# Attention in front of two expert layers: the pieces of the global rows move to another accumulation bank

## The chip, the cores and the metric

The kernel runs on one core of a Trainium2 chip. TensorE (PE in the profile, with PEld for its weight loads) multiplies matrices into PSUM, an accumulation memory of 8 banks; VectorE (DVE), ScalarE (ACT) and GpSimd (POOL) work element by element; SyncE (SP) issues the transfers. Each engine takes its own instructions in order, and engines wait for each other by semaphores. The metric is the device time of one execution in microseconds.

## The reference

Local rows attend to 32 global keys and to local keys within 32 positions; global rows attend to everything. Two dense layers follow: one with a leaky activation, and one with eight experts of equal capacity.

```python
k_all = np.concatenate([k_g, k_l], axis=2)
v_all = np.concatenate([v_g, v_l], axis=2)
s_g = scale * np.matmul(q_g, k_all.transpose(0, 1, 3, 2))
out_g = np.matmul(sm(s_g), v_all)
...
mask = np.abs(pos[:, None] - pos[None, :]) <= window
s_ll = np.where(mask, s_ll, -1000000000.0)
s_l = np.concatenate([s_lg, s_ll], axis=-1)
out_l = np.matmul(sm(s_l), np.concatenate([v_g, v_l], axis=2))
...
h = x @ w_in
g = np.maximum(h, 0.0) + alpha * np.minimum(h, 0.0)
x = g @ w_out
```

There are 4 batches of 8 heads, 512 local and 32 global rows each, with a head size of 64.

## The kernel before

A *unit* is a batch and two heads. Two units make a pair p, 8 in all, and a pair takes four steps j = 0 to 3; the running step is n = 4 p + j, from 0 to 34. What is issued in a step is written out by hand for TensorE, VectorE and ScalarE in `attention()`, so that each step works on several steps' data. In step n:

- `scores(p, j)`: the local scores of step n go into two banks `s` (L456). VectorE reduces them in four pieces, scaling, masking and taking the least (L462, an instruction and a read of its accumulator each); ScalarE exponentiates (L466).
- `dense.products(n)`: from step 12 on, half a column block of the first dense layer (h, L684, later L692), so that TensorE has other work.
- `wide_part(n)`: the global rows. They take a whole pair's four steps. j = 1: the pair's global scores, 512 columns in a bank of their own and 32 more (`gscores`, L522), their least (L529) and their exponential (L533). j = 3: the exponentials are transposed, four blocks in an own bank and two in `s` (`gtrans`, L545), and copied to `gt` (L546). j = 0 of the next pair: their product with the values (`gpv`, L555, 24 matmuls, each recorded as two in the trace), scaled on VectorE into `go` (L558). j = 2: that is turned (`gturn`, L565) and copied to the output (L566). All parts but the two with own banks use columns 256 to 511 of the *second scores bank* of the running step, `G[p]["s"][1]`.
- `pv(n - 2)` (L488), local product of step n - 2, into columns 0 to 255 of a bank `o`, which VectorE normalises in `norm` (L494, L496). `ptrans(n - 1)` (L474) transposes the exponentials of step n - 1, and ScalarE copies them to `pt` (L476). `oturn(n - 3)` (L503) turns the rows of step n - 3 into columns 256 to 511 of the `o` bank of the step before, and VectorE or ScalarE in turn copies them out (L505).

The global pieces leave their VectorE and ScalarE work in a list `soon`, which is emptied right after `wide_part`, before pv and norm. Between these, `fill("V", ...)` puts VectorE's part of the decoding of 64-bit weights (L87 to L94), whose raw blocks the SP queue loads (L80). Before step 12, TensorE also runs a few products of the unit matrix on the new `o` bank (L616). `dense.close` computes `al1` = 1 - alpha (L653) in step 13, from `ag`, which is loaded at L603.

There are two `s` banks from step 8 on, and two `o` banks. A bank `o` is used in its own step and the next, and is free again when the copy L505 of the next step has read it.

Of the kernel before, what the change touches and what calls it, by code (L numbers as in the profile page):

```python
# [9 lines left out]
F32 = mybir.dt.float32  # L10
# [4 lines left out]
AF = mybir.ActivationFunctionType  # L15
OP = mybir.AluOpType
# [3 lines left out]
BIG = 3.0e38  # L20
# [5 lines left out]
def tile_attention_moe_moe(ctx: ExitStack, tc: tile.TileContext, qkw, vw,  # L26
                           w_in, w_out, w_out_t, gate, w1, w2, out):
    nc = tc.nc
    V, A, P, T = nc.vector, nc.scalar, nc.gpsimd, nc.tensor
    B, H, S, D, SG = BHSDG  # L30
# [330 lines left out]
    with ExitStack() as at:  # L361
# [14 lines left out]
        def bank(shape, name):  # L376
            pool, tag = pY, "y"
            if name == "s" and wide[0]:
                pool, tag = pS, "s"
            elif name == "s":  # L380
                pool, tag = ((pS, "s"), (pS, "s"), (pH, "h1"), (pH, "h1"))[turn[0] % 4]
                turn[0] += 1
            elif name in ("t", "gs0", "gt0"):
                pool, tag = pX, "x"
            return pool.tile(shape, F32, name=name, tag=tag)
# [94 lines left out]
        def pv(p, j, o):  # L480
            d = G[p]
            d["o", j] = o
            for pr in range(2):
                for h, c in heads():
                    for w in range(2):
                        i = 4 * j + 2 * pr + w
                        for a in range(2):
                            T.matmul(o[lane(w, a), 128 * pr + D * h:128 * pr + D * h + D], d["t", j][:, 2 * pr + h, lane(w, a)],  # L488
                                     U[2 * p + a]["v"][:, i, c], start=True, stop=True)
# [20 lines left out]
        def glane(a, h):  # L510
            return slice(SG * (2 * a + h), SG * (2 * a + h + 1))

        def gscores(p, part):
            d = G[p]
            if part == 0:
                d["mx"] = gp.tile([128, 4], F32, name="gmx", bufs=2)
            mx = d["mx"]
            s = d["s"][1][:, 256:256 + SG] if part else bank([128, S], "gs0")
            for a in range(2):
                k = U[2 * p + a]["k"]  # L520
                x = k[:, WIN:2 * WIN] if part else k[:, GO:GE + WIN].rearrange("p (m c) -> p m c", c=3 * WIN)[:, :, :2 * WIN]
                T.matmul(s[64 * a:64 * a + 64], U[2 * p + a]["g"], x, start=True, stop=True)  # L522
            if part:
                to, x, z = gsc[:, 2 * WIN:3 * WIN], s, gzero.to_broadcast([128, SG])
            else:
                to = gsc[:, :GE + WIN - GO].rearrange("p (m c) -> p m c", c=3 * WIN)[:, :, :2 * WIN]
                x = s.rearrange("p (m c) -> p m c", c=2 * WIN)
                z = gzero.unsqueeze(2).to_broadcast([128, S // (2 * WIN), 2 * WIN])
            V.tensor_tensor_reduce(out=to, in0=x, in1=z, scale=-D ** -0.5, scalar=mx[:, 0:1] if part else BIG,  # L529
                                   op0=OP.add, op1=OP.min, accum_out=mx[:, part:part + 1])  # L530
            if part:
                d["p"] = gp.tile([128, GE - GO], F32, name="gpr")
                A.activation(out=d["p"], in_=gsc[:, :GE - GO], func=AF.Exp, bias=mx[:, 1:2], scale=-1.0, accum_out=mx[:, 2:3])  # L533
                P.tensor_scalar(mx[:, 2:3], mx[:, 2:3], 1e-9, None, op0=OP.add)
                later.append(lambda: V.reciprocal(mx[:, 3:4], mx[:, 2:3]))

        def gtrans(p, part):
            d = G[p]
            n = 2 if part else 4
            t = d["s"][1][:, 256:].rearrange("p (n q) -> p n q", q=128) if part else bank([128, n, 128], "gt0")  # L540
            if not part:
                d["t"] = gp.tile([128, len(GW), 128], F32, name="gt")
            for i in range(n):
                o = kpos(GW[4 * part + i]) - GO
                T.transpose(t[:, i], d["p"][:, o:o + KW], ident)  # L545
            soon.append(lambda: (V.tensor_copy if part else A.copy)(d["t"][:, 4 * part:4 * part + n], t))  # L546

        def gpv(p, s):
            d = G[p]
            o = s[:, 256:256 + D]  # L550
            for n, w in enumerate(GW):
                r = slice(96 if w == NQ - 2 else 0, 128)
                for h, c in heads():
                    for a in range(2):
                        T.matmul(o[glane(a, h)], d["t"][r, n, glane(a, h)], U[2 * p + a]["v"][r, w, c],  # L555
                                 start=n == 0, stop=n == len(GW) - 1)
            d["o"] = gp.tile([128, D], F32, name="go")
            soon.append(lambda: V.tensor_scalar(d["o"], o, d["mx"][:, 3:4], None, op0=OP.mult))  # L558

        def gturn(p, s):  # L560
            d = G[p]
            o = s[:, 256:256 + 2 * SG]
            i = ident.rearrange("p (a h q) -> p h a q", a=2, h=2)
            for h, r in heads():
                T.matmul(o[r], d["o"], i[:, h], start=True, stop=True)  # L565
            soon.append(lambda: V.tensor_copy(d["x"][:, :, :SG], o.rearrange("p (a q) -> p a q", q=SG)))  # L566
# [10 lines left out]

        later, soon, at_out = [], [], [None]

        def wide_part(n):  # L580
            p, j = divmod(n, STEPS)
            last = n - STEPS * NU // 2
            if last >= 0:
                s = bank([128, 512], "s") if last in (0, 1) else None
            else:
                s = G[p]["s"][1]
            if j == 1 and last < 0:
                gscores(p, 0)
                gscores(p, 1)
            if j == 3:  # L590
                gtrans(p, 0)
                gtrans(p, 1)
            if p and j == 0:
                gpv(p - 1, s)
            if p and (j == 2 or last == 1):
                gturn(p - 1, s)

        def attention():
            N = STEPS * NU // 2
            for n in range(N + 3):  # L600
                p, j = divmod(n, STEPS)
                if n == SOLO - 1:
                    nc.sync.dma_start(out=ag, in_=gate)  # L603
                wide[0] = n >= SOLO
                dense.turn(n)
                if n < N:
                    scores(p, j)
                while later:
                    later.pop(0)()
                dense.close(n)  # L610
                fill("V", 2)
                o = None
                if 2 <= n < N + 2:
                    o = bank([128, 512], "o")
                    for _ in range((2, 0, 2, 2)[j] if n < BEG else 0):
                        T.matmul(o[:, :128], ident, ident, start=True, stop=True)  # L616
                dense.products(n)
                if n < N + 2:
                    wide_part(n)
                while soon:  # L620
                    soon.pop(0)()
                fill("V", 2 if n >= SOLO and n % 3 == 0 else 1 if n < SOLO else 0)
                if 2 <= n < N + 2:
                    v, j2 = divmod(n - 2, STEPS)
                    pv(v, j2, o)
                    norm(v, j2)
                if 1 <= n <= N:
                    ptrans(*divmod(n - 1, STEPS))
                if n >= 3:
                    oturn(*divmod(n - 3, STEPS))  # L630
                if p and j == 3:
                    gout(p - 1)
                if n > 2:
                    fill("A", 2)
                yield 0
            while later:
                later.pop(0)()
            gout(NU // 2 - 1)

        class dense:  # L640
# [8 lines left out]
                dense.over = []  # L649

            def close(n):
                if n == BEG + 1:
                    V.tensor_scalar(al1, al, -1.0, 1.0, op0=OP.mult, op1=OP.add)  # L653
                if n == BEG - 3:
                    dense.x = [gx.tile([128, KD, CH], F32R, name=nm) for nm in ("xh", "xl")]
                    dense.g = [gt_.tile([128, KH, CH], F32R, name=nm, tag=nm) for nm in ("ghi", "glo")]
                if n in (BEG - 2, BEG - 1):
                    k = slice(0, 2) if n == BEG - 2 else slice(2, KD)
                    split(dense.x[0][:, k], dense.x[1][:, k], XB[0][:, k, :CH], lo_eng=P)
                for f, ps, neg in dense.neg:  # L660
                    g = gh_.tile([128, CH], F32, name="g")
                    V.scalar_tensor_tensor(g, neg, al1[:, f:f + 1], ps, op0=OP.mult, op1=OP.add)
                    split(dense.g[0][:, f], dense.g[1][:, f], g, lo_eng=P)
# [157 lines left out]
    with ExitStack() as mo:  # L821
# [903 lines left out]
        for k in range(E):  # L1725
            n = 0.0
# [103 lines left out]
```

## Time and profile before

| | us |
|---|---|
| runs | 803.5, 808.19, 808.4 |
| median | 808.19 |
| profiled execution | 804.26 |
| its span, first to last instruction | 802.2 |
| PE busy | 758.6 (95%) |
| DVE busy | 483.3 (60%) |
| ACT busy | 404.0 (50%) |
| POOL busy | 413.6 (52%) |

The time of an execution holds its span and what lies around it. The attention with its steps takes the first 140 us or so; after it come the first dense layer, the choice of the experts' rows and the second layer. Busy shares are means over all of these.

### The profile page before, as it was taken

To read this page: it belongs to the slowest core of one execution; us is meant where nothing else is said; L and a number is where in the kernel's file an instruction comes from. 1 tells how busy PE (TensorE), PEld (TensorE's weight loads), DVE (VectorE), ACT (ScalarE), POOL (GpSimd) and SP (SyncE) were. 2 spreads that over 40 slices of the span, in tenths; PEclk is the share of its full clock that TensorE was granted. 3 is DMA by queue.
4 is the path that set the end of the run, shared out by engine and by line. 5 is a ranking of instruction groups with operands and counts; after the bars stand their busy time and mean duration, and the time that the engine had idled before them with its cause. 6 is when DMAs were issued, how large, how long until landed. Compare 5 with 4: busy or idle time off the path is not lost. (4 is left out here: it accounts for less than half of the span.)

```text
span 802.2 us, 21108 instructions
## 1 busy us (share of the span) xinstructions
PE 758.6 (95%) x8258; PEld 695.8 (87%) x8258; DVE 483.3 (60%) x1672; ACT 404.0 (50%) x1018; POOL 413.6 (52%) x384
## 2 busy tenths in 40 slices
PE   6888889999999999899999999999999999999996
PEld 4656667999998999798898999998889999999994
DVE  3788887375664754266655566766677777652220
ACT  5787888345544453454565234423555454544430
POOL 2233333023211332865587349355899987788511
PEclk9999999999999999999999999999999999999999
DMA  8989896431434342126543957316466666466510
GB/s 335 317 301 310 304 314 233 168 122 50 125 110 135 107 145 98 57 64 217 196 141 113 322 199 229 97 33 186 140 194 213 206 185 203 139 190 218 172 41 29
DMA packets 59516, 139.56 MB, mean 174 GB/s; under 512 B 5400, under 2 KB 23000, under 8 KB 58393
## 3 DMA queue, kind: packets, MB, share of 16 engines
q1 hardware_dynamic: 56489, 129.30, 49.6%
q0 software_dynamic: 2928, 8.92, 3.1%
q8 instruction: 65, 1.06, 0.5%
q14 instruction: 34, 0.28, 0.1%
HBM read 113.68 MB, written 24.51 MB: 172 GB/s over the span
## 5 line engine op out<-in xcount | busy, mean ns | idle before, releaser
L74 POOL TENSOR_TENSOR m<-raw,m 128x1024 fp32r<-128x1024 f32 x64 | 152.1, 2401 | 10.8 <-ACT m L73 9.6
L74 POOL TENSOR_TENSOR glo<-g,ghi 128x272 fp32r<-128x272 f32 x64 | 55.1, 860 | 137.6 <-ACT ghi L73 119.4
L1427 PE MATMUL h<-xsh,m 128*128 128x272 f32 x512 | 104.6, 294 | 0.7 <-DVE sbs L1193 0.7
L882 PE MATMUL h<-op,quad 128*128 128x272 f32 x672 | 90.4, 294 | 4.3 <-ACT g L907 2.3
L882 PEld LDWEIGHTS h<-op,quad 128*128 128x128 f32 x672 | 86.6, 191 | 8.4 <-ACT g L907 2.8
L73 ACT CAST m<-raw 128x1024 fp32r<-128x1024 f32 x64 | 65.8, 1048 | 54.9 <-DMA raw<-in_moe_w_dram 37.9
L1447 PE MATMUL h<-hh,m 128*128 128x272 f32 x448 | 92.1, 295 | 0.0
L1582 PE MATMUL h<-gr,wh 128*128 128x272 f32 x448 | 90.8, 296 | 0.0
L251 PE MATMUL y<-ghi,wout 128*128 128x272 f32 x448 | 87.0, 290 | 0.5 <-ACT ghi L73 0.5
L211 PE MATMUL h<-xh,win 128*128 128x272 f32 x448 | 86.2, 290 | 0.0
L1427 PEld LDWEIGHTS h<-xsh,m 128*128 128x128 f32 x512 | 82.0, 188 | 1.4 <-DVE sbs L1193 1.0
L1427 PE MATMUL h<-xsl,m 128*128 128x272 f32 x256 | 73.8, 291 | 0.0
L251 PEld LDWEIGHTS y<-ghi,wout 128*128 128x128 f32 x448 | 70.8, 188 | 2.4 <-issue 1.7
L1447 PEld LDWEIGHTS h<-hh,m 128*128 128x128 f32 x448 | 72.1, 189 | 0.4 <-ACT m L73 0.4
L1582 PEld LDWEIGHTS h<-gr,wh 128*128 128x128 f32 x448 | 71.2, 189 | 0.9 <-ACT gr L73 0.4
L211 PEld LDWEIGHTS h<-xh,win 128*128 128x128 f32 x448 | 70.7, 188 | 0.2 <-DVE g L217 0.2
L1447 PE MATMUL h<-hl,m 128*128 128x272 f32 x224 | 66.3, 296 | 0.0
L251 PE MATMUL y<-glo,wout 128*128 128x272 f32 x224 | 64.7, 289 | 1.5 <-POOL glo L74 1.5
L1582 PE MATMUL h<-gr,wl 128*128 128x272 f32 x224 | 65.7, 293 | 0.0
L211 PE MATMUL h<-xl,win 128*128 128x272 f32 x224 | 64.4, 288 | 0.0
L74 POOL TENSOR_TENSOR gr<-gback,gr 128x272 fp32r<-128x272 f32 x48 | 36.2, 778 | 39.9 <-ACT gr L73 39.5
L466 ACT ACTIVATE pr<-pr,mx 128x128 f32<-128x128 f32 x128 | 49.7, 392 | 12.4 <-DVE mx L462 12.4
(326 smaller groups left out, 1775.9 us busy)
## 6 DMA issues: line engine op xcount, KB each, us to landing
raw<-in_moe_w_dram SPq DMA_DIRECT2D x64, 512.0 KB, 3.7
vv<-in_v_dram SPq DMA_DIRECT2D x28, 512.0 KB, 6.3
qk<-in_qk_dram SPq DMA_DIRECT2D x28, 360.0 KB, 7.1
raw<-in_moe_w_in_dram SPq DMA_DIRECT2D x16, 512.0 KB, 3.9
raw<-in_moe_w_out_dram SPq DMA_DIRECT2D x16, 512.0 KB, 3.5
xs<-xb SPq DMA_DIRECT2D x16, 272.0 KB, 6.4
xpart<-xd SPq DMA_DIRECT2D x32, 136.0 KB, 2.5
xb<-xs SPq DMA_DIRECT2D x4, 1088.0 KB
```

Of the source, the lines that this page charges most:

```text
L73: a = A.copy(hi, src)
L74: return a, (lo_eng or V).tensor_tensor(lo, src, hi.bitcast(F32), op=OP.subtract)
L211: T.matmul(ps, WI[w][:, k, fs], x[:, k], start=i == 0, stop=i == 3 * KD - 1)
L251: T.matmul(ps, WO[w][:, f, ds_], x[:, f], start=f == 0 and i == 0, stop=f == KH - 1 and i == 2)
L466: A.activation(out=sc, in_=sc, func=AF.Exp, bias=d["mx", j][:, ii:ii + 1], scale=-1.0, accum_out=d["sm", j][:, ii:ii + 1])
L882: T.matmul(ps, w[a][kk][:, q * 128:(q + 1) * 128], x[:, b, kk], start=fresh and m == 0, stop=m == 5, skip_group_check=not fresh)
L1427: T.matmul(ps, d["w1"][w][:, kk, f * 128:(f + 1) * 128], x[:, kk], start=kk == 0 and i == 0, stop=kk == KD - 1 and i == 2)
L1447: T.matmul(ps, d["w2"][w][f][:, ms], x[:, f], start=i == 0, stop=i == 3 * K3 - 1)
L1582: T.matmul(ps[j], (woh, wol)[w][f][:, ds_], x, start=f == 0 and a == 0, stop=f == KH - 1 and a == 2)
```

## The change

The global pieces are put into columns 256 to 511 of the step's `o` bank, which `wide_part` now gets as an argument; it is taken from step 1 on. The global product is done by units: unit 0 in j = 0 and unit 1 in j = 1, 12 matmuls each, each with its own scaling of 64 partitions. The small part of the global scores is multiplied before pv, the wide part after it. `soon` is emptied after pv and norm. `al1` is computed in step 7 and `ag` is issued in step 1.

```diff
-            s = d["s"][1][:, 256:256 + SG] if part else bank([128, S], "gs0")
+            s = so[:, 480:480 + SG] if part else bank([128, S], "gs0")
...
-            t = d["s"][1][:, 256:].rearrange("p (n q) -> p n q", q=128) if part else bank([128, n, 128], "gt0")
+            t = so[:, 256:].rearrange("p (n q) -> p n q", q=128) if part else bank([128, n, 128], "gt0")
...
-        def gpv(p, s):
+        def gpv(p, s, units_):
...
-                    for a in range(2):
+                    for a in units_:
...
-            soon.append(lambda: V.tensor_scalar(d["o"], o, d["mx"][:, 3:4], None, op0=OP.mult))
+            if units_[0] == 0:
+                d["o"] = gp.tile([128, D], F32, name="go")
+            b = slice(2 * SG * units_[0], 2 * SG * (units_[-1] + 1))
+            soon.append(lambda: V.tensor_scalar(d["o"][b], o[b], d["mx"][b, 3:4], None, op0=OP.mult))
...
+            last = n >= STEPS * NU // 2
+            if p and j < 2 and not (last and j):
+                gpv(p - 1, s, range(2) if last else (j,))
+            if p and j == (1 if last else 2):
+                gturn(p - 1, s)
+            if j == 1 and not last:
+                soon.append(gscores(p, 1, s))
             if j == 3:
                 gtrans(p, 0)
-                gtrans(p, 1)
...
+                gtrans(p, 1, s)
...
-                if n == SOLO - 1:
+                if n == 1:
                     nc.sync.dma_start(out=ag, in_=gate)
...
-                    wide_part(n)
+                    wide_part(n, o)
+                if 2 <= n < N + 2:
+                    pv(*divmod(n - 2, STEPS), o)
+                    norm(*divmod(n - 2, STEPS))
+                if j == 1 and n < N:
+                    soon.insert(0, gscores(p, 0))
                 while soon:
                     soon.pop(0)()
...
-                if 2 <= n < N + 2:
-                    v, j2 = divmod(n - 2, STEPS)
-                    pv(v, j2, o)
-                    norm(v, j2)
...
-                if n == BEG + 1:
+                if n == SOLO - 1:
                     V.tensor_scalar(al1, al, -1.0, 1.0, op0=OP.mult, op1=OP.add)
```

On TensorE, steps 8 and 9 (j = 0 and j = 1 of pair 2) read before, with `s<-vv,gt` the global product, `gs` the wide and `s<-qk 64x32` the small global scores:

```order
L456 MATMUL s<-qk 32x128 x16
L616 MATMUL o<-ident 128x128 x2
L555 MATMUL s<-vv,gt 32x64 x24
L488 MATMUL o<-vv,pt 32x64 x16
L474 MATMUL t<-ident,pr 128x128 x4
L503 MATMUL o<-ident,on 128x128 x2
L456 MATMUL s<-qk 32x128 x16
L522 MATMUL gs_859<-qk 64x512 x2
L522 MATMUL s<-qk 64x32 x2
```

and now:

```order
L456 MATMUL s<-qk 32x128 x16
L616 MATMUL o<-ident 128x128 x2
L558 MATMUL o<-vv,gt 32x64 x12
L488 MATMUL o<-vv,pt 32x64 x16
L474 MATMUL t<-ident,pr 128x128 x4
L503 MATMUL o<-ident,on 128x128 x2
L456 MATMUL s<-qk 32x128 x16
L558 MATMUL o<-vv,gt 32x64 x12
L522 MATMUL o<-qk 64x32 x2
L488 MATMUL o<-vv,pt 32x64 x16
L522 MATMUL gs_883<-qk 64x512 x2
L474 MATMUL t<-ident,pr 128x128 x4
```

Half of the global product has gone to the next step, its bank is `o`, and the wide scores stand behind pv.

On VectorE, step 13 (j = 1 of pair 3) reads before, from the last read of L462 to the first L462 of step 14:

```order
L462 ISA mx 128x1
L653 TENSOR_SCALAR al_71<-ag 128x16
L87 TENSOR_SCALAR mag<-mag 128x512
L90 TENSOR_SCALAR mag<-mag 128x512
L529 ISA gsc,gmx<-gs_1214,gzero 128x8x64
L529 ISA gmx 128x1
L529 ISA gsc,gmx<-s,gzero,gmx 128x32
L529 ISA gmx 128x1
L494 RECIPROCAL sm<-sm 128x4
L496 TENSOR_TENSOR on<-o,sm 128x256
L505 COPY xb<-o 128x4x2x32
L462 ISA pr,mx<-s,mask 128x128
```

and now:

```order
L462 ISA mx 128x1
L87 TENSOR_SCALAR mag<-mag 128x512
L90 TENSOR_SCALAR mag<-mag 128x512
L494 RECIPROCAL sm<-sm 128x4
L496 TENSOR_TENSOR on<-o,sm 128x256
L531 ISA gsc,gmx<-gs_1238,gzero 128x8x64
L531 ISA gmx 128x1
L563 TENSOR_SCALAR go<-o,gmx 64x64
L531 ISA gsc,gmx<-o,gzero,gmx 128x32
L531 ISA gmx 128x1
L505 COPY xb<-o 128x4x2x32
L462 ISA pr,mx<-s,mask 128x128
```

The norm (L494, L496) has moved ahead of the global reductions (now L531), a scaling of unit 1 stands between these, and L653 has left the step.

## Rows read from the trace of the kernel before

**Rows 1.** Windows: stretch, its length, busy us by engine, granted clock, DMA share, GB/s.

```profile
core 0: us, PE busy (x) PEld busy (x) DVE busy (x) ACT busy (x) POOL busy (x), PEclk, DMA share, GB/s
60.00:100.00 40.00, 33.48 (x810) 25.09 (x814) 33.14 (x133) 31.61 (x111) 14.13 (x21) 1.00 0.90 307
100.00:140.00 40.00, 35.62 (x880) 27.37 (x868) 32.94 (x149) 33.78 (x120) 14.65 (x22) 1.00 0.80 273
160.00:300.00 140.00, 137.92 (x1081) 134.39 (x1080) 88.64 (x153) 66.81 (x155) 39.75 (x47) 1.00 0.37 112
```

**Rows 2.** Waits of PE, 22 to 146 us: us in total, times, longest.

```profile
PE o L488 <- issue: 4.1, 3, 1.8
PE s L555 <- ACT pr L466: 2.8, 2, 1.6
PE s L555 <- DVE mx L462: 1.7, 4, 0.6
PE t L474 <- issue: 1.4, 1, 1.4
PE s L565 <- DVE mx L462: 1.4, 4, 0.9
...
PE s L545 <- DVE mx L462: 1.0, 2, 0.7
PE s L456 <- issue: 0.9, 1, 0.9
...
PE s L555 <- ACT mag L85: 0.3, 1, 0.3
```

**Rows 3.** Waits of DVE in the same stretch.

```profile
DVE pr L462 <- PE s L456: 6.9, 13, 1.0
DVE on L496 <- PE o L488: 2.6, 6, 1.0
DVE go L558 <- PE s L555: 2.5, 2, 2.1
...
DVE xb L566 <- PE s L565: 1.0, 2, 0.6
```

**Rows 4.** Timeline of PE, step 16 (j = 0): start, us, instruction, idle before.

```profile
72.76 0.29 PE L684 MATMUL h<-xh,win 128*128 128x272 f32 x1
74.27 1.10 PE L555 MATMUL s<-vv,gt 128*32 128x64 f32 x48 [1.22 <-ACT pr L466]
75.31 0.65 PE L488 MATMUL o<-vv,pt 128*32 128x64 f32 x32
75.89 0.66 PE L474 MATMUL t<-ident,pr 128*128 128x128 f32 x4
```

**Rows 5.** Timeline of DVE, end of step 15 to start of step 17.

```profile
72.87 0.41 DVE L505 COPY xb<-o 128x256 f32<-128x256 f32 x1
...
74.04 0.08 DVE L462 DVE_READ_ACCUMULATOR2_ANT mx<- 128x1 f32 x1
...
75.64 0.17 DVE L494 RECIPROCAL sm<-sm 128x4 f32<-128x4 f32 x1
76.03 0.42 DVE L496 TENSOR_TENSOR on<-o,sm 128x256 f32<-128x256 f32 x1 [0.21 <-PE o L488]
77.40 0.29 DVE L462 CUSTOM_DVE_ANT_0 pr<-s,mask 128x128 f32<-128x128 f32 x1 [0.95 <-PE s L456]
```

**Rows 6.** Groups by line, 0 to 150 us: busy us, mean ns, idle before, releaser.

```profile
L533 ACT ACTIVATE gpr<-gsc,gmx 128x736 f32<-128x736 f32 x8 | 7.3, 910 | 8.9 <-DVE gmx L529 8.9
...
L558 DVE TENSOR_SCALAR go<-s,gmx 128x64 f32<-128x64 f32 x8 | 2.3, 282 | 2.6 <-PE s L555 2.5
...
L653 DVE TENSOR_SCALAR al<-ag 128x16 f32<-128x16 f32 x1 | 1.0, 987 | 0.0
```

**Rows 7.** Timeline of all engines, steps 13 and 14.

```profile
63.78 0.59 ACT L476 COPY pt<-t 128x512 f32<-128x512 f32 x1 [0.27 <-PE t L474]
...
65.85 0.65 PE L488 MATMUL o<-vv,pt 128*32 128x64 f32 x32
```

**Rows 8.** Timeline of PE where the attention ends.

```profile
147.30 0.39 PE L692 MATMUL y<-ghi,wout 128*128 128x272 f32 x1
```

More of the change, by code (lines that the diff above doesn't have):

```diff
@@ L511, in glane, with gscores @@
             return slice(SG * (2 * a + h), SG * (2 * a + h + 1))
-        def gscores(p, part):
+        def gscores(p, part, so=None):
             d = G[p]
-            if part == 0:
+            if part:
                 d["mx"] = gp.tile([128, 4], F32, name="gmx", bufs=2)
             mx = d["mx"]
-            s = d["s"][1][:, 256:256 + SG] if part else bank([128, S], "gs0")
+            s = so[:, 480:480 + SG] if part else bank([128, S], "gs0")
             for a in range(2):
@@ L528, in gscores, with least, gtrans @@
                 z = gzero.unsqueeze(2).to_broadcast([128, S // (2 * WIN), 2 * WIN])
[L529 to L537, printed above, removed]
+            def least():
+                V.tensor_tensor_reduce(out=to, in0=x, in1=z, scale=-D ** -0.5, scalar=mx[:, 0:1] if part else BIG,
+                                       op0=OP.add, op1=OP.min, accum_out=mx[:, part:part + 1])
+                if part:
+                    d["p"] = gp.tile([128, GE - GO], F32, name="gpr")
+                    A.activation(out=d["p"], in_=gsc[:, :GE - GO], func=AF.Exp, bias=mx[:, 1:2], scale=-1.0, accum_out=mx[:, 2:3])
+                    P.tensor_scalar(mx[:, 2:3], mx[:, 2:3], 1e-9, None, op0=OP.add)
+                    later.append(lambda: V.reciprocal(mx[:, 3:4], mx[:, 2:3]))
+            return least
+        def gtrans(p, part, so=None):
             d = G[p]
             n = 2 if part else 4
-            t = d["s"][1][:, 256:].rearrange("p (n q) -> p n q", q=128) if part else bank([128, n, 128], "gt0")
+            t = so[:, 256:].rearrange("p (n q) -> p n q", q=128) if part else bank([128, n, 128], "gt0")
             if not part:
@@ L553, in gpv @@
                 for h, c in heads():
-                    for a in range(2):
+                    for a in units_:
                         T.matmul(o[glane(a, h)], d["t"][r, n, glane(a, h)], U[2 * p + a]["v"][r, w, c],
                                  start=n == 0, stop=n == len(GW) - 1)
-            d["o"] = gp.tile([128, D], F32, name="go")
-            soon.append(lambda: V.tensor_scalar(d["o"], o, d["mx"][:, 3:4], None, op0=OP.mult))
+            if units_[0] == 0:
+                d["o"] = gp.tile([128, D], F32, name="go")
+            b = slice(2 * SG * units_[0], 2 * SG * (units_[-1] + 1))
+            soon.append(lambda: V.tensor_scalar(d["o"][b], o[b], d["mx"][b, 3:4], None, op0=OP.mult))
         def gturn(p, s):
@@ L578, in tile_attention_moe_moe, with wide_part @@
         later, soon, at_out = [], [], [None]
-        def wide_part(n):
+        def wide_part(n, s):
             p, j = divmod(n, STEPS)
[L582 to L589, printed above, removed]
+            last = n >= STEPS * NU // 2
[5 more added lines that the diff above has]
+                soon.append(gscores(p, 1, s))
             if j == 3:
                 gtrans(p, 0)
-                gtrans(p, 1)
[L593 to L596, printed above, removed]
+                gtrans(p, 1, s)
         def attention():
@@ L612, in attention @@
                 o = None
-                if 2 <= n < N + 2:
+                if 1 <= n < N + 2:
                     o = bank([128, 512], "o")
-                    for _ in range((2, 0, 2, 2)[j] if n < BEG else 0):
+                    for _ in range((2, 0, 2, 2)[j] if n < BEG and n > 1 else 0):
                         T.matmul(o[:, :128], ident, ident, start=True, stop=True)
@@ L622, in attention @@
                 fill("V", 2 if n >= SOLO and n % 3 == 0 else 1 if n < SOLO else 0)
-                if 2 <= n < N + 2:
-                    v, j2 = divmod(n - 2, STEPS)
-                    pv(v, j2, o)
-                    norm(v, j2)
                 if 1 <= n <= N:
```

## The prediction

> **What bounds the kernel now.** I read first the table of windows [rows 1]. While the attention runs, up to some 140 us, TensorE is busy 33 to 36 of every 40 us, VectorE about 33, and the DMA engines 0.80 to 0.90 of the time; no engine is full. Right behind, TensorE is busy 137.9 of 140 us. So a microsecond won in the attention moves everything behind it forward by about one, and one won on another engine behind it is worth nothing. The clock is granted in full in all of these windows, so it takes no part.
>
> Then the waits of TensorE in that stage, steps 4 to 33 [rows 2]. Two kinds matter. Where the releaser is called "issue", no semaphore is shown: 4.1 + 1.4 + 0.9 = 6.4 us. The change touches none of that. The others stand in front of the global pieces: L555 (product) 2.8 + 1.7 + 0.3 = 4.8 us, L565 (turning) 1.4, L545 (transposes) 1.0, together 7.2 us. The releaser of L565, L545 and part of L555 is L462, VectorE's reduction of the scores of the *same* step. L555 reads no score. It waits since it writes columns 256 and on of a bank whose first 256 columns L462 is still reading. In step 16 this can be followed [rows 4, 5]: the last product h ends at 72.76 + 0.29 = 73.05, L555 starts at 74.27, and the last accumulator read of L462 is at 74.04 to 74.12. The row names ACT L466 there, which reads no PSUM bank; the true releaser is the L462 just before.
>
> The third view is VectorE's own waits [rows 3]: it waits for TensorE's scores 6.9 us, for pv 2.6, for the global product 2.5 and its turning 1.0, together 13.0 us. The two engines hold each other up in turns. After the 1.22 us of L555 in step 16, VectorE idles 0.21 before its norm and 0.95 before the next L462 [rows 5]. A stall of TensorE is worth only what VectorE idles behind it.
>
> **The waits that go.** In the output bank a global piece waits for the last reader of that bank, the copy L505 of the step before, and no longer for L462. L505 is late too at times: in step 16 it ends at 72.87 + 0.41 = 73.28, so that 0.23 of the 1.22 us would stay, a fifth. Of the 7.2 us I let 5.8 go. The ceiling on what that returns is VectorE's idle time for TensorE less what the issue gaps cause of it: 13.0 - 6.4 = 6.6 us. So nearly all 5.8 could return, but the idle time need not lie in the same steps. I take four fifths, 4.7 us; the ends are 0 and 6.6.
>
> The Trainium skill ("PSUM — Partial Sum Buffer", section "PSUM bank collisions raise a hardware error") says that PSUM must be guarded by bank and quadrant of partitions, and that another address of the same bank still collides. The wait of L555 for a reader of other columns agrees with that. The rule also speaks against the change: the piece now shares its bank with pv, so VectorE may read it only after pv. By that alone, with no stall returned, the sum would be that of the second case below.
>
> **The product in two halves.** TensorE's matmuls stay as many; 1.04 us in step j = 0 (74.27 to 75.31 [rows 4]) become about 0.52 there and 0.52 in j = 1. That moves work between two steps and costs TensorE nothing. VectorE gains a scaling: one per pair becomes two, except for the last pair, 7 more. Half as many partitions, but the same 64 elements in a row; the nearest row is 0.282 us [rows 6]. 7 x 0.28 = 2.0 us. Where VectorE waits anyway it costs nothing: I count half, 1.0 us, ends 0 and 2.0.
>
> **The order in j = 1.** The wide global scores used to come right behind the products. Now half a global product (0.52) and pv (75.31 to 75.89, 0.58 [rows 4]) stand ahead: TensorE has them 1.1 us later. VectorE uses the time for the norm that was pulled ahead of them (0.17 + 0.42, some 0.6 us [rows 5]). That leaves 0.5 us in each of 7 pairs, 3.5 us if VectorE is the later engine every time. Because TensorE no longer halts in the other steps it comes into j = 1 ahead; I count a third, 1.1 us, ends 0 and 3.5. In the other steps the norm is merely taken before the copies, and the same work lies behind it.
>
> **1 - alpha sooner.** L653 took 0.99 us [rows 6], in step 13, where it stands between L462 and the decoding and delays the global reduction. Moved to step 7 it lies in front of decoding that has slack. Half of it is a gain, 0.5 us, ends 0 and 1.0. The load of ag that it reads moves up on SP's queue, past one qk piece and one raw block that are needed steps later. I put it at nothing; if a later block failed to hide it, its issue is one small transfer more in front of them, under a microsecond once. Some other loads and stores swap neighbours on SP; the order on ScalarE and GpSimd is unchanged. The last steps, 32 and 33, swap one free bank for another: nothing.
>
> **Sum.** -4.7 + 1.0 + 1.1 - 0.5 = -3.1 us. The profiled execution took 804.26 us (span 802.2, 2.1 us outside). It lies low among the runs: 803.5, 808.19 and 808.4. From it the sum gives 801.2, from the median 805.1. I state 803, between the two, since nothing in the profile tells which level a run takes.
>
> **The rivals.**
> *VectorE takes over (0.20).* Every global read now stands behind the norm, and the norm behind pv. If VectorE is then the later engine in all j = 1 steps, the costs are at their ends, 2.0 + 3.5 = 5.5, against 4.7 + 0.5. This also covers that the waits only change their name, from L462 to L505. For it: VectorE is busy 33 of 40 us already. Against it: 13.0 us of its idle time wait for TensorE. The time is +0.3: 804.6 from the profile, 808.5 from the median; no change.
> *The coupling dissolves (0.17).* TensorE runs a step ahead, all 6.6 us return, L653 gives 1.0 and the added work hides: -7.6, 796.7 or 800.6. Against it: the DMA engines, at 0.90, would have to deliver the pairs sooner, and the issue gaps stay.
> *ScalarE falls behind, slower (0.08).* One mechanism, in j = 1: the exponential of the global scores (L533, 0.91 us, and it already waits 8.9 us in 8 executions [rows 6]) stands on ScalarE's queue ahead of the copy of pt (L476), and pv of the next step reads pt. In step 13 that copy ended at 63.78 + 0.59 = 64.37 and pv came at 65.85 [rows 7], 1.48 us later. If the global minimum comes over 1.5 us later, TensorE waits there. At 2.5 us later it loses 1.0 in each of 7 pairs; with the scalings at 2.0 against 4.7 that is +4.3: 808.6 or 812.5. I expect 0.5 to 1.1 us later, below the point, hence the small chance.
>
> **How the numbers follow.** The forecast keeps 0.55. The range must reach the second and third rivals: 796 (the dissolved coupling from the low level) to 811 (most of the slower case, and no change at the high level). About 1% is what a measurement of this kernel can tell from no change, so the lines are 800.1 and 816.3. Faster: a third of the forecast, at the low level or with its terms at their good ends (0.18), and two thirds of the dissolved coupling (0.11), 0.29. Slower by that much needs more than the ScalarE case at the median level: 0.04. The rest, 0.67, is within 1%.
>
> **What the new profile would show.** The waits of the global pieces for L462 should be gone, and what is left in front of the product should name L505. VectorE's waits for the scores should fall from 6.9 us to 3 or so, and its norm's wait for pv may rise above 2.6. The issue gaps should stay near 6.4 us. The end of the attention, the first y<-ghi,wout of L692 at 147.30 before [rows 8], should come about 3 us earlier, and everything behind it keep its length. It would be wrong if VectorE idles more in j = 1 than it gains elsewhere, if TensorE waits there for pt, or if qk becomes a releaser in the middle of the stage.

## The result, and the profile after

The changed kernel takes 811.6 us (median of 20 runs, 805.97 to 816.19), the kernel before, in 20 runs beside it, 806.24 (801.25 to 811.21). The ratio is 1.0057 with an interval of 1.0035 to 1.0079: slower by 0.6%, some 4.6 us, where 0.4% less had been forecast, and the median lies 0.6 us above the stated range. Ratios here and below leave out the runs that were slow as a whole, four of the kernel before (812.7 to 817.6 us) and one of a variant (2479.5 us). The profiled execution took 807.28 us against 804.26, with a span of 805.3 against 802.2.

The lines keep their order but not their numbers: the global product is now L558, the global scores L522, their least L531, their exponential L535, the transposes L548, the turning L570, the first dense layer's products L685 and L693.

The first question is where the time is lost. This is TensorE's timeline at the end of the attention; `y<-ghi,wout` stood at 147.30 before [rows 8].

```profile
152.17 0.40 PE L693 MATMUL y<-ghi,wout 128*128 128x272 f32 x1
```

So 4.9 us are lost up to there, and 1.8 of them come back behind it (653.1 us to the end of the span, 654.9 before). The windows from 22 us to that instruction say in what form; first the kernel before:

```profile
22.00:147.30 125.30, 108.40 (x2669) 81.19 (x2669) 100.19 (x424) 97.36 (x337) 40.83 (x61) 1.00 0.82 280
```

and the kernel after:

```profile
22.00:152.17 130.17, 115.70 (x2647) 86.53 (x2645) 102.39 (x428) 95.22 (x334) 38.61 (x61) 0.97 0.79 269
```

TensorE's idle time fell, from 125.30 - 108.40 = 16.9 to 14.5 us. Its *busy* time rose by 7.3 us, though its instructions are the same. A loss of 7.3 - 2.4 = 4.9.

The clock has a part in this pair of profiles: it was granted at 0.97 here and at 1.00 before. Two stretches of 3.4 us at half clock (last section) cost at most half of their length, 3.4 us together. The kernel before has such a stretch behind its first y (windows 335 to 340 and 340 to 345, granted 0.85 and 0.80), which costs it at most 1.75 us: about as much as the 1.8 that seem to come back. These are estimates from the windows; the price of the change is read from the runs, further down, not from this pair.

The groups by line, 0 us to the same two points, name the one that grew (busy us and mean ns behind the bar, then the idle time before it). Before:

```profile
L555 PE MATMUL s<-vv,gt 128*32 128x64 f32 (+1 forms) x384 | 8.3, 222 | 4.8 <-ACT pr L466 2.8 <-DVE mx L462 1.7 <-ACT mag L85 0.3
```

After:

```profile
L558 PE MATMUL o<-vv,gt 128*32 128x64 f32 (+1 forms) x384 | 14.8, 222 | 4.9 <-DVE xb L505 4.7 <-ACT xb L505 0.2
```

As many records, and each as long (222 ns), yet 6.5 us more. Records overlap, and in the halves they overlap less. And the wait in front of them hasn't gone, it has another name. The waits of TensorE after, from 22 us to its first y (the rows of [rows 2] hold for the kernel before up to its first y too):

```profile
PE o L558 <- DVE xb L505: 4.7, 3, 1.6
PE o L616 <- ACT xb L505: 2.9, 2, 1.6
PE o L488 <- ACT pt L476: 1.7, 6, 0.4
PE o L488 <- issue: 1.0, 2, 0.7
PE o L570 <- ACT xb L505: 0.8, 1, 0.8
PE o L570 <- DVE xb L505: 0.7, 1, 0.7
PE o L616 <- DVE xb L505: 0.7, 2, 0.3
PE o L548 <- ACT xb L505: 0.5, 1, 0.5
...
PE t L474 <- issue: 0.2, 1, 0.2
PE s L456 <- issue: 0.2, 1, 0.2
...
PE o L558 <- ACT xb L505: 0.2, 1, 0.2
```

The waits of the global pieces were 4.8 + 1.4 + 1.0 = 7.2 us; they are 4.7 + 0.2 + 0.8 + 0.7 + 0.5 = 6.9. Other pieces waited for L505 before, too:

```profile
PE o L616 <- ACT xb L505: 1.3, 2, 0.7
PE o L616 <- DVE xb L505: 0.6, 2, 0.3
PE o L488 <- ACT xb L505: 0.5, 1, 0.5
```

With these 2.4 us there were 9.6 us of waits for L462 and L505 together; now all of TensorE's waits for L505, with L616 (the unit matrix), are 10.5. None has gone. What did shrink is what the change doesn't touch, "issue": 6.4 before, 1.0 + 0.2 + 0.2 = 1.4 now. New is the wait of pv for `pt`.

In step 16, shown before in [rows 4, 5], TensorE now does this:

```profile
71.20 0.29 PE L685 MATMUL h<-xh,win 128*128 128x272 f32 x1
73.09 1.00 PE L558 MATMUL o<-vv,gt 128*32 128x64 f32 x24 [1.61 <-DVE xb L505]
74.02 0.65 PE L488 MATMUL o<-vv,pt 128*32 128x64 f32 x32
```

and VectorE this:

```profile
70.53 0.42 DVE L496 TENSOR_TENSOR on<-o,sm 128x256 f32<-128x256 f32 x1
70.87 0.41 DVE L549 COPY gt<-o 128x256 f32<-128x256 f32 x1
71.20 0.68 DVE L92 SCALAR_TENSOR_TENSOR mag<-raw,mag 128x512 int32<-128x512 int32 x1
71.92 0.69 DVE L94 SCALAR_TENSOR_TENSOR mag<-raw,mag 128x512 int32<-128x512 int32 x1
72.53 0.42 DVE L505 COPY xb<-o 128x256 f32<-128x256 f32 x1
```

The bank that the product needs comes free with L505, and L505 stands on VectorE's queue behind the norm, the copy of the transposes and two decoding instructions of 0.7 us each. TensorE halts 1.61 us, more than the 1.22 of before.

VectorE's own waits, as in [rows 3]:

```profile
DVE on L496 <- PE o L488: 4.5, 7, 1.1
DVE mag L87 <- ACT mag L85: 4.0, 7, 1.1
DVE pr L462 <- PE s L456: 3.7, 7, 0.9
DVE g L663 <- ACT neg L648: 3.2, 7, 1.3
DVE gsc L531 <- PE gs L522: 2.4, 5, 0.6
DVE gmx L537 <- POOL gmx L536: 1.6, 6, 0.3
```

They sum to 19.4 us. The waits for TensorE's scores fell as forecast (6.9 to 3.7), but in their place stand waits for ScalarE (`mag`, `neg`). ScalarE, in its turn, waits for VectorE's global minimum; first the row of before, then, in a fence of its own, that of after:

```profile
ACT gpr L533 <- DVE gmx L529: 7.8, 7, 1.5
```

```profile
ACT gpr L535 <- DVE gmx L531: 18.5, 7, 3.6
```

1.1 us for each of 7 pairs before, 2.6 now.

### The profile page after: what moved, and what is told of

It is laid out like the page before. It is cut to its first block, busy times and chain, and to the rows that moved or that the text cites. A ratio compares the mean times of both kernels' runs of the same rounds, so it can differ in the third digit from the quotient of the medians.

```text
span 805.3 us, 21133 instructions
## 1 busy us (share of the span) xinstructions
PE 764.1 (95%) x8258; PEld 700.0 (87%) x8258; DVE 486.0 (60%) x1679; ACT 401.7 (50%) x1018; POOL 411.5 (51%) x384
## 5 line engine op out<-in xcount | busy, mean ns | idle before, releaser
L883 PE MATMUL h<-op,quad 128*128 128x272 f32 x672 | 88.6, 290 | 3.6 <-ACT g L908 2.3
```

Source lines behind the costliest of these rows:

```text
L883: T.matmul(ps, w[a][kk][:, q * 128:(q + 1) * 128], x[:, b, kk], start=fresh and m == 0, stop=m == 5, skip_group_check=not fresh)
```

## The experiments

Three theories stood at first. **A, the bank comes free late:** what is lost is the halt of up to 1.6 us in front of L558, and with it the clock, which in this profile fell to half behind two of the three halts. **B, ScalarE is held up:** the exponential waits 1.5 us longer for the minimum, and the copy of `pt` stands behind it. **C, the halves are dear:** 12 matmuls of one unit take as long as 24 of both. Each kernel ran 12 times, against 35 runs of the kernel before on the same chip. Line numbers of the variants differ by a few from those of the changed kernel.

**The changed kernel again**, without an edit.

> The changed kernel itself, so that the variants sent with it have it on the same chip. Both theories expect what was measured, some 4 to 5 us over the kernel before, and in the profile one or more lumps of 1.6 us in which TensorE stands before the global product (L558) for L505, with the granted clock at 0.5 in a stretch behind each lump.

1.0050 (1.0019 to 1.0081), first y at 152.70: the loss repeats. The mean granted clock of its runs was 0.9944, that of the kernel before 0.9925. So the clock is no reason for the loss that the runs show.

**The copies first (A).** The decoding is put behind the copies.

```diff
                     soon.pop(0)()
-                fill("V", 2 if n >= SOLO and n % 3 == 0 else 1 if n < SOLO else 0)
...
                     oturn(*divmod(n - 3, STEPS))
+                fill("V", 2 if n >= SOLO and n % 3 == 0 else 1 if n < SOLO else 0)
```

> The changed kernel with the second decoding call of each step behind the copy L505 instead of ahead of it. Theory A (the output bank is freed late, since decoding stands ahead of L505 on VectorE; TensorE then stands still in one lump and its clock falls): the wait of L558 for L505 falls from 4.7 us to under 2, fewer stretches at a clock of 0.5 before 150 us, and 3 to 4 us less than the changed kernel. Theory B (in j = 1 ScalarE stands for the global minimum, 18.5 us against 7.8, and its later copies hold up the others): no more than 1 us less.

1.0065 (1.0032 to 1.0099). In front of the product 3.9 us of waits are left of 4.9, the profile has no stretch at half clock, and its first y lies at 148.96; the time of the 12 runs is none the better for it. So the half clock of the changed kernel's profile doesn't explain the loss. The edit moved waits more than it removed them: all of TensorE's waits for L505 up to the first y sum to 9.1 us here, against 10.5. What the lateness of L505 costs as a whole this run doesn't show.

**The wide scores first (B).** The wide global scores and their least go back ahead of pv.

```diff
             if j == 1 and not last:
-                soon.append(gscores(p, 1, s))
+                small_ = gscores(p, 1, s)
+                gscores(p, 0)()
+                soon.append(small_)
...
-                if j == 1 and n < N:
-                    soon.insert(0, gscores(p, 0))
```

> The changed kernel with the wide global scores multiplied and reduced ahead of pv and norm, as before the change; only the small part stays behind pv. Theory B: ScalarE's wait for the minimum falls from 18.5 us to 10 to 12, and the time by 2 to 3 us. Theory A: the lumps at L558 stay at 4 to 5 us and the time is within 1 us of the changed kernel.

1.0046 (1.0009 to 1.0083). ScalarE's wait for the minimum fell only from 18.5 to 15.8 us, since the small scores' least still stands behind the norm. The edit didn't remove the cost in question, so it tells little.

**The exponential behind (B).** The exponential and the two small instructions that follow it are issued after the copies of the step.

```diff
-                    A.activation(out=d["p"], in_=gsc[:, :GE - GO], func=AF.Exp, bias=mx[:, 1:2], scale=-1.0, accum_out=mx[:, 2:3])
-                    P.tensor_scalar(mx[:, 2:3], mx[:, 2:3], 1e-9, None, op0=OP.add)
-                    later.append(lambda: V.reciprocal(mx[:, 3:4], mx[:, 2:3]))
+                    behind.append((d, mx))
...
-                while later:
+                while later and j == 3:
                     later.pop(0)()
...
                     oturn(*divmod(n - 3, STEPS))
+                while behind:
+                    d, mx = behind.pop(0)
+                    A.activation(out=d["p"], in_=gsc[:, :GE - GO], func=AF.Exp, bias=mx[:, 1:2], scale=-1.0, accum_out=mx[:, 2:3])
+                    P.tensor_scalar(mx[:, 2:3], mx[:, 2:3], 1e-9, None, op0=OP.add)
+                    later.append(lambda mx=mx: V.reciprocal(mx[:, 3:4], mx[:, 2:3]))
```

> The changed kernel with ScalarE's exponential of the global scores behind the copies of its step, and the reciprocal of its sum in j = 3. Theory B: ScalarE's wait for the minimum falls under 5 us, VectorE's waits for ScalarE (L87 4.0 and L663 3.2 us) fall by half, and the time by 3 to 4 us. Theory A: the lumps at L558 stay at 4 to 5 us and the time falls by no more than 1 us.

1.0014 (0.9984 to 1.0044), no longer slower than the kernel before. ScalarE's wait for the minimum is down to 0.5 us. VectorE's waits for ScalarE hardly changed, though (`mag` 3.6, `neg` 2.8 us): these are not the exponential's work. The waits of pv for `pt` are gone: of the kernels with the pieces in the output bank, all seven profiles with the exponential ahead have 1.0 to 2.2 us of them, all four with it behind none.

**The whole product (C).** Both units in j = 0 again, in the output bank.

```diff
-            if p and j < 2 and not (last and j):
-                gpv(p - 1, s, range(2) if last else (j,))
+            if p and j == 0:
+                gpv(p - 1, s, range(2))
```

> The changed kernel with the whole global product in j = 0 again, both units together; all else as changed. Theory C (the product of one unit writes two of the four groups of 32 output columns, and TensorE's 12 matmuls of a unit take as long as 24 of both, 0.92 us against 1.04 in the traces, so that halving costs 0.8 us in each of 7 pairs): L558 falls from some 14 us to 8.3, the steps j = 1 from 5.1 to 4.2, and the time by 4 to 6 us, to the kernel before or under it. Theory B (ScalarE stands for the minimum): no more than 1 to 2 us, since the minimum still stands behind pv and norm.

1.0029 (0.9991 to 1.0068), first y at 153.79 in a profile with four stretches at half clock. The product's group is back at its old size:

```profile
L558 PE MATMUL o<-vv,gt 128*32 128x64 f32 (+1 forms) x384 | 8.9, 229 | 5.5 <-DVE xb L505 4.8 <-issue 0.7
```

5.9 us less work than in the changed kernel, but only some 2 us of time by the ratios. Its runs had a mean granted clock of 0.9898, the lowest of all; the comparison at equal clock below gives more. Issue gaps grew at the same time: 6.1 us of them up to the first y, where the changed kernel had 1.4.

**The kernel before, its product by units (C alone).** The loop over units becomes the outermost one; nothing else changes.

```diff
-            for n, w in enumerate(GW):
-                r = slice(96 if w == NQ - 2 else 0, 128)
-                for h, c in heads():
-                    for a in range(2):
+            for a in range(2):
+                for n, w in enumerate(GW):
+                    r = slice(96 if w == NQ - 2 else 0, 128)
+                    for h, c in heads():
```

> The kernel before with one edit: in the global product the loop over the two units is outermost, so that the same 24 matmuls run as 12 of unit 0 and then 12 of unit 1, in the same step and bank. Theory C: the group L555 grows from 8.3 us to 14 or 15 and the time by 3 to 6 us. If the halves cost nothing by themselves: L555 stays at 8.3 us and the time within 1 us of the kernel before.

1.0066 (1.0031 to 1.0100). Same matmuls, same bank, same step: this order alone makes the kernel before as slow as the changed one. Its group and two rows of its timeline:

```profile
L555 PE MATMUL s<-vv,gt 128*32 128x64 f32 (+1 forms) x384 | 16.2, 230 | 4.7 <-ACT pr L466 3.1 <-DVE mx L462 1.3 <-ACT mag L85 0.3
...
97.42 1.90 PE L555 MATMUL s<-vv,gt 128*32 128x64 f32 x48 [0.17 <-DVE mx L462]
99.24 0.65 PE L488 MATMUL o<-vv,pt 128*32 128x64 f32 x32
```

From the product's start to the next instruction 1.82 us. The kernel before has, after the same wait of 0.17 us:

```profile
92.20 1.01 PE L555 MATMUL s<-vv,gt 128*32 128x64 f32 x48 [0.17 <-DVE mx L462]
93.14 0.65 PE L488 MATMUL o<-vv,pt 128*32 128x64 f32 x32
```

0.94 us. C is shown.

**Whole product and exponential behind (B and C).** The edits of "The exponential behind" and "The whole product" together.

> The changed kernel with the whole product in j = 0, and the exponential of the global scores behind the copies of its step on ScalarE (reciprocal in j = 3). If theories B and C both hold and add up: 2 to 3 us under the whole product alone, and 3 to 5 us under the kernel before. If they overlap: as the whole product alone.

0.9964 (0.9932 to 0.9997). Faster than the kernel before, for the first time. The product's group is 8.3 us, the wait for the minimum 1.2, the wait of the product for L505 2.9.

**These two and the wide scores first.**

> As the run with the whole product and the exponential behind, and the wide global scores again ahead of pv and norm. With the exponential behind the copies nothing waits for the minimum soon, so it should be within 1 us of that run; if VectorE's wait for the wide scores mattered, 1 to 2 us less.

0.9968 (0.9938 to 0.9999), not to be told from the kernel above.

**`ag` and 1 - alpha put back** in the changed kernel.

```diff
-                if n == 1:
+                if n == SOLO - 1:
                     nc.sync.dma_start(out=ag, in_=gate)
...
-                if n == SOLO - 1:
+                if n == BEG + 1:
                     V.tensor_scalar(al1, al, -1.0, 1.0, op0=OP.mult, op1=OP.add)
```

> The changed kernel with 1 - alpha and its load where they were (step 13, load at step 7). My term was 0.5 us, ends 0 and 1.0: the time should be within 1 us of the changed kernel, L653 of 1 us standing in step 13 again.

1.0060 (1.0031 to 1.0089), beside 1.0057 and 1.0050 with them moved. The move is worth nothing that these runs show.

**The kernel before, its exponential behind.** The edit of "The exponential behind", in the kernel before.

> The kernel before with only the exponential of the global scores moved behind the copies of its step (reciprocal in j = 3). It tells where the 3 us come from by which the versions with the whole product and this move beat the kernel before. If from this move alone: 2 to 3 us under the kernel before here too, and the other bank is worth nothing. If from the bank: within 1 us of the kernel before, whose ScalarE waited 7.8 us for the minimum and not 15 to 18.

1.0031 (0.9999 to 1.0064): no gain there. So the gain of the two fast kernels is not one that the kernel before could have had by that edit alone.

**The copies first** in the kernel with the whole product, the exponential behind and the wide scores first, and **in the one with the whole product alone**.

> The version with the whole product, the wide scores ahead of pv and the exponential behind, and with the second decoding call behind the copy L505 in addition. Theory A as far as it is left: the wait of the product for L505 falls from 2.9 us to under 1.5 and the time by 1 to 2 us against that version, to 4 or 5 us under the kernel before. If VectorE's whole work per step is what counts, not its order: within 1 us of that version.

> The changed kernel with the whole product in j = 0 and the second decoding call behind L505. The whole product alone came out 2 to 3 us over the kernel before at a mean granted clock of 0.990, the lowest of all. If the lumps of TensorE's idle time at L558 (4.8 us in 3 waits) bring the clock down: these shrink to under 2.5, the mean clock rises to 0.993 or more and the time falls by 2 to 4 us. If not, clock and time stay.

0.9971 (0.9942 to 1.0000) and 1.0016 (0.9989 to 1.0044). The wait of the product for L505 falls to 1.6 us in both; against 0.9968 and 1.0029 without the edit the times stay within their intervals. Here, too, the waits went to other pieces in the bank: all waits of TensorE for L505 up to the first y are 8.5 us without the edit and 7.9 with it on the first base, 10.0 and 10.1 on the second. Which piece waits is worth little; what L505 holds up as a whole is not priced by these runs.

The kernels side by side. The columns from "first y" on are from one profile each: clock is the granted clock and busy is TensorE's from 22 us to the first y, by the windows; issue is the sum of its rows of that name in the waits of that stretch; other idle is the rest of the stretch. "Equal clock" is an estimate from the runs. Each run has its mean granted clock on record. A straight line through the 244 runs that the ratios of the experiments use, with one slope for all and a level of its own for each kernel and set, gives 0.72 us more for each 0.001 of clock less. The column has the us over the kernel before of the same set at the same clock by that line, good to about 1.3 us; for the change it is that of its twelve runs beside the variants.

| product, exponential | ratio | equal clock | first y | clock | busy | issue | other idle |
|---|---|---|---|---|---|---|---|
| before | 1 | 0 | 147.30 | 1.00 | 108.4 | 6.4 | 10.5 |
| before, by units | 1.0066 | +5.8 | 155.19 | 0.98 | 118.6 | 1.8 | 12.8 |
| before, exponential behind | 1.0031 | +1.8 | 151.87 | 0.97 | 111.4 | 8.3 | 10.2 |
| halves, ahead (the change) | 1.0057 | +4.8 | 152.17 | 0.97 | 115.7 | 1.4 | 13.1 |
| halves, behind | 1.0014 | +2.3 | 151.93 | 0.96 | 117.4 | 3.2 | 9.3 |
| whole, ahead | 1.0029 | +0.3 | 153.79 | 0.95 | 114.1 | 6.1 | 11.6 |
| whole, ahead, copies first | 1.0016 | +1.7 | 147.76 | 0.99 | 108.8 | 4.8 | 12.2 |
| whole, behind | 0.9964 | -1.5 | 149.09 | 0.97 | 111.2 | 8.5 | 7.4 |
| whole, behind, wide first | 0.9968 | -2.3 | 146.35 | 0.97 | 108.9 | 6.6 | 8.8 |
| the same, copies first | 0.9971 | -0.4 | 146.33 | 0.99 | 109.4 | 6.6 | 8.4 |

The profiles have more or fewer stretches at half clock, so that the point of the first y and the ratio don't follow each other row by row, and busy time holds the clock's share. At equal clock the kernels sort all the same: halves with the exponential ahead, +4.8; either of the two put right, +2.3 and +0.3 (+1.7 with the copies first); both, -0.4 to -2.3. The other kernels with halves and the exponential ahead lie at +5.8 (copies first), +4.3 (wide scores first) and +6.0 (1 - alpha put back). Halves are dearer in busy time and have few issue gaps; with the exponential behind, in the output bank, the other idle time is lowest.

## Why the prediction was wrong

**The steps that failed** are two. The first is the one on the product: "That moves work between two steps and costs TensorE nothing." I counted matmuls and gave each half the half of 1.04 us. A half takes as long as the whole. The product writes four groups of 32 partitions, two units by two heads, and the loop takes the four in turn; a unit alone has two of them. Two pieces of the same length show the rate, the first out of a whole product of the kernel before,

```profile
92.35 0.62 PE L555 MATMUL s<-vv,gt 128*32 128x64 f32 x30
```

the second out of a half of the changed one,

```profile
93.74 0.61 PE L558 MATMUL o<-vv,gt 128*32 128x64 f32 x15
```

30 records against 15. So in each of 7 pairs some 0.9 us were added, 14.8 - 8.3 = 6.5 us in all. Put into the sum at its full size, that alone turns -3.1 into +3.4. The Trainium skill has the rule that I did not look for ("TensorEngine Tiling (Array Packing)", section "Key Properties"): tiles work independently, and different ones can load weights and multiply in parallel. With 32 columns it counts four tiles (section "Available Configurations"), of which a half uses two; the trace agrees with it, by 30 records to 15. What the runs show is the price of the order. A rival stays open: a half also adds to each of its sums again after one other matmul instead of three, and no run tells that from the two idle column groups.

Not all of it reached the end. The six profiles with halves in that bank show 1.1 to 4.1 us of issue gaps, the five with the whole product 4.8 to 8.5 (the changed kernel itself 1.4 in one profile and 2.8 in the other): TensorE was slower where it would have stood idle anyway. The price in time was 0.3% (1.0057 against 1.0029) to 0.5% (1.0014 against 0.9964), some 2 to 4 us, with intervals that overlap; in the kernel before, 0.66%. At equal clock it is 4.5 and 3.8 us, each good to some 2 us, and 5.8 in the kernel before. That gaps and work trade in this way is read from profiles; no run had the gaps taken away.

This step is not the whole miss. With the whole product the change is at 1.0029 and 1.0016, and neither interval reaches down to the 0.996 of the forecast. The second step that failed is the largest term, -4.7 us for waits that go: they stayed.

**The waits that go.** I let 5.8 of 7.2 us go, with a fifth left to L505. In the profile 0.3 went, and none with L616 counted. The name was right, the size wrong. I held the end of L505 against the time at which TensorE came before. VectorE's work ahead of that copy in step 15 is the same in both kernels, in another order; before, up to the copy in [rows 5]:

```profile
70.59 0.42 DVE L546 COPY gt<-s 128x256 f32<-128x256 f32 x1
...
71.65 0.69 DVE L94 SCALAR_TENSOR_TENSOR mag<-raw,mag 128x512 int32<-128x512 int32 x1
...
72.53 0.42 DVE L496 TENSOR_TENSOR on<-o,sm 128x256 f32<-128x256 f32 x1
```

L505 ends at 73.28 before and at 72.95 now, 0.33 us sooner. TensorE is done with its last product h at 73.05 before and at 71.49 now, 1.56 us sooner, and stands until the copy is done. Its halts of 1.6 us look like the culprit in the profile. The copies put first removed one us of 4.9 from them in the changed kernel and 3.2 of 4.8 with the whole product, and neither became measurably faster; but since TensorE then waited for L505 with other pieces, what all these waits cost stays open.

**What returned.** "The issue gaps should stay near 6.4 us" failed too, 1.4. That the scores' waits would fall to 3 or so came about (3.7), as did the norm's rise above 2.6 (4.5), and VectorE's idle time only changed owners (19.7 us in all rows of that view before, 19.4 after). The rival that the waits merely change their name was nearer than the forecast on this point, but its price of +0.3 still counts the 4.7 us as returned, and so does every other case, also where the text says "with no stall returned". With nothing returned its own terms give 2.0 + 3.5 - 0.5 = +5.0, beside a measured +4.6; that these are close is partly luck, as the halves are not in it.

**The order in j = 1.** Forecast +1.1 us, with ScalarE as a rival that decides from 1.5 us on, and the minimum 0.5 to 1.1 us later. ScalarE waited 1.5 us longer for it (18.5 / 7 against 7.8 / 7), and pv waited for `pt` 1.7 us in all, which the prediction had named as a sign of being wrong. One pair of steps where that is seen, TensorE at step 29,

```profile
134.83 0.98 PE L558 MATMUL o<-vv,gt 128*32 128x64 f32 x24
135.75 0.31 PE L522 MATMUL o<-qk 128*64 128x32 f32 x4
135.98 0.65 PE L488 MATMUL o<-vv,pt 128*32 128x64 f32 x32
136.57 1.08 PE L522 MATMUL gs<-qk 128*64 128x512 f32 x4
...
140.57 0.65 PE L488 MATMUL o<-vv,pt 128*32 128x64 f32 x32 [0.30 <-ACT pt L476]
```

and ScalarE,

```profile
139.04 0.91 ACT L535 ACTIVATE gpr<-gsc,gmx 128x736 f32<-128x736 f32 x1 [2.88 <-DVE gmx L531]
139.95 0.56 ACT L476 COPY pt<-t 128x512 f32<-128x512 f32 x1
```

ScalarE stands for 2.88 us, the copy of `pt` ends 0.06 us before pv starts. The half of the product that I had put at 0.52 us in front of the wide scores is 135.75 - 134.83 = 0.92: the first error fed this one. Taking the exponential out of the way was worth 0.4% with halves (1.0057 to 1.0014) and 0.65% with the whole product (1.0029 to 0.9964). The intervals of each of these two pairs overlap; at equal clock it is 2.5 and 1.8 us, where in the kernel before the same edit costs 1.8. So this rival, at 0.08, was a good part of the loss, and it and the halves add up roughly: from 0.9964 with neither to 1.0057 with both. That it works through `pt` is shown in part: those waits are gone in every profile with the exponential behind, but they were 1 to 2 us.

**The small terms.** The scalings came to 15 instead of 8 and 4.2 us instead of 2.3 on VectorE, the 2.0 us foreseen. 1 - alpha was put at -0.5; it showed nothing. What lies behind the attention kept its length but for 1.8 us, about as much as the half clock there can have cost the kernel before.

**The idea itself** gained nothing by itself. With the pieces in the output bank and the product whole, but the exponential where it was, the kernel is at 1.0029 and 1.0016, at equal clock 0.3 and 1.7 us over the kernel before, where -3.1 was forecast. Only with the exponential behind, an edit that the change didn't have, it is at 0.9964 to 0.9971: some 2.5 us under before by the ratios, 0.4 to 2.3 at equal clock, with intervals that end at 0.9997 to 1.0000. These three, whose intervals overlap, are the best versions found. The kernel with the whole product had the lowest mean clock of all (0.9898), and with the copies first it had 0.9926 and 1.0016; at equal clock the edit shows no gain. What stays open is why the clock differs.

## What to carry to other kernels

Here a group of small matmuls was priced by whether its loop kept all four of the array's column groups in turn, not by their number; before splitting one, look which groups each half writes, and read the pitch from the start of the group to the start of the next instruction. Moving a buffer to another bank exchanges one reader for another: price the new reader by when it ends and by when the waiting engine will come *after* the change, which is sooner once its old waits are gone. And an instruction whose input comes later holds everything behind it on its queue; where it has slack itself, issue it last.

## What the runs showed of the hardware that was not expected

Half the matmuls in the same time (24 records in 0.93 us from 73.09 to 74.02, 48 in 0.94 from 92.20 to 93.14), as told above.

The granted clock. Windows of the changed kernel around the halt in step 16, with the columns of [rows 1]:

```profile
70.00:74.86 4.86, 3.25 (x96) 2.59 (x90) 4.33 (x17) 3.53 (x12) 1.50 (x2) 1.00 0.89 310
74.86:78.27 3.41, 3.41 (x44) 2.70 (x42) 2.50 (x14) 2.72 (x13) 0.99 (x2) 0.50 1.04 400
78.27:82.00 3.73, 3.73 (x72) 2.31 (x71) 2.18 (x6) 0.81 (x5) 0.22 (x1) 1.00 0.95 347
```

Behind the halt of 1.61 us that ended at 73.09, TensorE got half its clock, 1.2 instead of 2.4 GHz, for 3.41 us, and did 44 matmul records in them where the 3.73 us after have 72. A second such stretch begins at 95.34, behind the halt that ended at 93.68. The kernel before had halts of 1.6 and 1.8 us in the same stage [rows 2] and a granted clock of 1.00 there [rows 1]. So such a halt does not always bring it, and no run here settled what else it takes.
